# Fused local attention and feed-forward on one core: the weights' low parts move from GpSimd to VectorE, and blocks 0 to 5 scale their value products instead of their probabilities

## The chip, the core and the metric

The kernel runs on one core of a Trainium2 chip. The core has five engines, each with an instruction queue of its own that is worked off in order: TensorE (PE in the profile; its weight loads are listed apart as PEld), VectorE (DVE), ScalarE (ACT), GpSimd (POOL) and SyncE (SP), which here only issues DMA transfers. The metric is the time of one execution on the device in microseconds (us). The median of three runs before the change is 757.61 us.

## What is computed

The reference has two stages. The first is attention over 4 batches of 8 heads with 768 positions and 64 columns a head, in which a query sees the first 8 keys of its batch and the last 96 keys up to itself, with a bias that grows with distance:

```python
scores = scale * np.matmul(q, k.transpose(0, 1, 3, 2))
bias = -slopes[:, None, None] * dist[None, :, :]
scores = np.where(keep, scores + bias[None], -1000000000.0)
scores = scores - np.max(scores, axis=-1, keepdims=True)
a = np.exp(scores)
a = a / (np.sum(a, axis=-1, keepdims=True) + 1e-09)
attn_out = np.matmul(a, v).astype(np.float32)
```

The second takes the 3072 tokens of 512 columns that come out, x, through one feed-forward layer of width 2048:

```python
h = x @ w_in
g = h * (1.0 / (1.0 + np.exp(-h)))
out = (g @ w_out).astype(np.float32)
```

q, k and v come as 32-bit floats; w_in and w_out come as 64-bit floats, 8 MB each.

## The kernel before

**Attention** is cut into 24 blocks of 128 queries (six for each batch), `i` in the code, and each block into four pairs of heads, `hp`. A block needs 232 keys: 96 from the block before, the 8 global ones and its own 128; the first block of a batch needs only its own 128. For each block TensorE turns k and q (`turn`, L448), and for each pair of heads it makes the scores (L528 for blocks 0 to 5, L500 from block 6 on). VectorE adds the bias and finds the top (`top_of`, L540), ScalarE takes the exponential and its row sums (`expo`, L548), VectorE adds 1e-9 to the two sums of the pair and inverts them (`guard` L555, `inverse` L559), and `norm` (L565 to L574) scales the two heads' probabilities: one on GpSimd (L572) and one on VectorE (L574) for the first 16 pairs, that is blocks 0 to 3, and both on VectorE from block 4 on. TensorE turns the scaled probabilities (`turn_p`, L583), ScalarE moves them to SBUF as `pt` (L589), and TensorE multiplies them by v (`values`, L603). There v is the stationary operand, 64 columns a head, and `pt` streams 128 columns past it, so the result `pav` has the features of a head in its rows and the queries in its columns. ScalarE and VectorE split it into a high and a low part (`x_high` L615, `x_low` L618).

**The weights** come in 32 pieces of 512 KB, `n`, even ones from w_in and odd ones from w_out (`stage`, L364). VectorE puts a 32-bit float together from the halves of each 64-bit one in three steps (`conv1` L368, `conv2` L374, `conv3` L380), ScalarE rounds it to the reduced format of fast products (`conv_hi`, L387), and GpSimd subtracts this from the full value for the low part (`conv_lo`, L391).

**The feed-forward layer** takes two blocks at a time as a group `g` (12 groups) and the layer's width in 16 steps `f`. TensorE makes the hidden part from three products of high and low parts (`moe_h`, L723, 12 products a step), ScalarE takes the tanh (L729), VectorE makes the gate (`moe_gate`, L733), ScalarE rounds it (`moe_high`, L737) and the low part is subtracted (`moe_low`, L742: on GpSimd for groups 0 and 1 with f below 4, else on VectorE). TensorE multiplies by w_out (`moe_o`, L749, 6 products a step) into two PSUM banks that the group holds for all 16 steps. Step f needs the weights 2f and 2f + 1 with both their parts, so groups 0 and 1 run beside the conversion; block 6 and the later ones start their scores only when it is over, since their low parts of q take buffers of the staged weights.

**The order** of every engine's queue is fixed before the launch. The program lists its operations with an engine, a cost in ns, a rank, what they depend on and which buffers they take. `Plan.run` plays them through: whenever an engine is free it gives it the ready operation of the lowest rank whose buffers are to be had (`room`). So a changed cost or a changed engine alters the order of everything behind it. Where TensorE would have nothing to do in the first 60 us of this play, small products on zeros are put in (`filler`, L861). Eight PSUM banks are shared out by kind: output of the layer (`po`), values (`av`), scores (`s`), hidden part (`h`) and two kinds of turned data (`tp`, `tq`).

Of the kernel before, what the change touches and what calls it, by code (L numbers as in the profile page):

```python
# [10 lines left out]
F32 = mybir.dt.float32  # L11
# [6 lines left out]
ALU = mybir.AluOpType  # L18
# [3 lines left out]
P = 128  # L22
# [3 lines left out]
C1 = NPREV + NG  # L26
# [7 lines left out]

    C0=14, CR=1, LW=1, LB=5, QB=3.5, RI=0.1, RN=0, RP=0.2, RM=0, RV=1.2, RQ=0.1, RB=3, LK=-25, LAG=1,

    BP=(4, 3), NA=(0, 0), NP=(16, 0), PL=4, NX=20, CF=2, AHEAD=5, CN=4, I0=6, QS='ACT',
)


# [7 lines left out]
class Plan:  # L48
# [28 lines left out]
    def op(self, eng, cost, rank, emit, deps=(), uses=(), lat=None):  # L77
        o = dict(eng=eng, cost=int(cost), rank=rank, emit=emit, uses=list(uses), lat=lat,
                 need=0, ready=0, then=[], n=len(self.ops))
        for d in deps:  # L80
            if d is not None:
                d["then"].append(o)
                o["need"] += 1
        for b in o["uses"]:
            b.left += 1
        self.ops.append(o)
        return o
# [83 lines left out]
def attn_moe(ctx, tc, q, k, v, n_global, n_local, w_in, w_out, out):  # L171
# [216 lines left out]

    def conv_lo(n):
        _, hi, lo = weights(n)  # L390
        nc.gpsimd.tensor_sub(lo, st["f", n], hi.bitcast(F32))  # L391

    o_w, o_l = [], [None, None]
    for n in range(2 * NFC):
        rank = PAR["C0"] + PAR["CR"] * n
        a, m, x = [] if lent(n) is not None else [Buf("big")], Buf("mid"), lent(n)
        o = op("DMA", 1456, rank - PAR["LW"], (lambda n=n: stage(n, "w")), [o_l[x]] if not a else (), a, PAR["DL"])
        o = op("DVE", 335, rank, (lambda n=n: conv1(n)), [o], [*a, m])
        o = op("DVE", 602, rank, (lambda n=n: conv2(n)), [o], [*a, m])
        o = op("DVE", 602, rank, (lambda n=n: conv3(n)), [o], [*a, m])  # L400
        if x is not None:
            o_l[x] = o
        o_wf = o
        hi = op("ACT", 520, rank, (lambda n=n: conv_hi(n)), [o] + (o_l if n >= 2 * NFC - 4 else []), [m])
        lo = op("POOL", 1225, rank, (lambda n=n: conv_lo(n)), [hi], [m])
        o_w.append((hi, lo))
    lo["caps"] = dict(pt=5)

# [123 lines left out]
    def top_of(i, hp, a):  # L532
        t = blk[i]
        if not a:
            t["p", hp] = sb3.tile([P, 2, WIN], F32, name="pe")
            t["sum", hp] = sb3.tile([P, 2], F32, name="sm")
            t["inv", hp] = sb3.tile([P, 2], F32, name="rs")
        h, n = 2 * hp + a, cols(i)[1]
        nm = NM[:, i * H + h:i * H + h + 1]
        nc.vector.tensor_tensor_reduce(  # L540
            t["p", hp][:, a, :n], t["s", hp][a][:, :n], B1[:, h] if i % NJ else B0[:, h],
            -SC, 3.0e38, ALU.add, ALU.min, nm,
        )
# [14 lines left out]
        t = blk[i]  # L558
        nc.vector.reciprocal(t["inv", hp], t["inv", hp])  # L559

    def norm_on(u, a):

        return "ACT" if u < PAR["NA"][a] else "POOL" if u < PAR["NP"][a] else "DVE"

    def norm(i, hp, a):  # L565
        t = blk[i]
        x = t["p", hp][:, a, :cols(i)[1]]
        eng = norm_on(NHP * i + hp, a)
        if eng == "ACT":
            nc.scalar.mul(x, x, t["inv", hp][:, a:a + 1])  # L570
        elif eng == "POOL":
            nc.gpsimd.tensor_mul(x, x, t["inv", hp][:, a:a + 1].to_broadcast(x.shape))  # L572
        else:
            nc.vector.tensor_scalar(x, x, t["inv", hp][:, a:a + 1], None, ALU.mult)  # L574

    def turn_p(i, hp, tp):
        t = blk[i]
# [17 lines left out]
    def values(i, hp, av):  # L595
        t = blk[i]
        t["av"] = bank(av, NHP, P)
        pav, pt = t["av"], t["pt", hp]
        for c in range(0 if i % NJ else 1, 2):
            for a in range(2):  # L600
                r = slice(a * D, (a + 1) * D)
                x = t["v"] if c else t["vp"]
                nc.tensor.matmul(  # L603
                    pav[r, hp], x[:, 2 * hp + a], pt[:P if c else C1, c, a],
                    start=not c or not i % NJ, stop=c == 1,
                )

    def x_part(i, x):
        g, jj = divmod(i, NB)
# [16 lines left out]
    for i in range(B * NJ):  # L626
# [47 lines left out]
        if j:  # L674
            o_v.append(op("DMA", 1183, rank - lr + 1, (lambda i=i: load_prev(i)), (), [kk["vp"]], PAR["DL"]))
        pav = Buf("av")
        last, o_m, pts = None, [], []
        for hp in range(NHP):
            u = NHP * i + hp
            stacked = i >= PAR["I0"]  # L680
            s, pe, pt, tp = [Buf("s") for _ in range(1 if stacked else 2)], Buf("pe"), Buf("pt"), Buf("tp")
            ks = [kk[x] for x in ("KH", "KL", "QH", "QL") + (("R",) if stacked else ())]
            n = cols(i)[1]
            o = op("PE", 432 if stacked else 640, u,
                   (lambda i=i, hp=hp, s=s, f=stack_scores if stacked else scores: f(i, hp, s)),
                   [x for y, x in ob.items() if i or y[1] <= hp < y[1] + NHP // 2] + [before.get("s") if stacked else None], s + ks)
            before["s"] = o_s[u] = o
            if u == PAR["HU"]:
                o["hold"] = 1
            o_e = []  # L690
            for a in range(2):
                x = op("DVE", 318 if j else 210, u, (lambda i=i, hp=hp, a=a: top_of(i, hp, a)),
                       [o, o_b[j == 0, hp], before.get("top") if stacked and not a else None], [s[a % len(s)], pe])
                if not a:
                    before["top"] = x
                o_e.append(op("ACT", ACT(n, 112) + 186, u, (lambda i=i, hp=hp, a=a: expo(i, hp, a)), [x], [pe]))
            o = op("DVE", 67, u - PAR["RI"], (lambda i=i, hp=hp: guard(i, hp)), o_e, [pe])
            o = op("DVE", 72, u - PAR["RI"], (lambda i=i, hp=hp: inverse(i, hp)), [o], [pe])
            cost = dict(ACT=380, DVE=250, POOL=640) if j else dict(ACT=293, DVE=196, POOL=400)
            o = [op(norm_on(u, a), cost[norm_on(u, a)], u - PAR["RN"], (lambda i=i, hp=hp, a=a: norm(i, hp, a)), [o], [pe])  # L700
                 for a in range(2)]
            o = op("PE", 438 if j else 220, u - PAR["RP"], (lambda i=i, hp=hp, tp=tp: turn_p(i, hp, tp)), o, [pe, tp])
            o_m.append(op("ACT", ACT(512 if j else 256), u - PAR["RM"], (lambda i=i, hp=hp: move_p(i, hp)), [o, before.get("move") if stacked else None], [tp, pt]))
            before["move"] = o_m[-1]
            pts.append(pt)
            if not stacked or hp == NHP - 1:
                last = op("PE", ((1860 if j else 980) if stacked else 540 if j else 290), u - PAR["RV"],
                          (lambda i=i, hp=hp, av=pav: values_of(i, hp, av)),
                          [*o_m, last] + o_v, [*pts, pav, xb[g]["xh"], xb[g]["xl"], kk["vn"]] + ([kk["vp"]] if j else []))
                o_m, pts = [], []  # L710
        hi = op("ACT", 478, u, (lambda i=i: x_high(i)), [last], [pav, xb[g]["xh"]])
        o_x[g].append(hi)
        o_x[g].append(op("DVE", 602, u, (lambda i=i: x_low(i)), [hi], [pav, xb[g]["xh"], xb[g]["xl"]]))
# [24 lines left out]

    def moe_low(g, f):
        mo["gl", g, f] = gl = sb2.tile([P, GT], F32R, name="gl")  # L740
        eng = nc.gpsimd if g < 2 and f < PAR["PL"] else nc.vector
        eng.tensor_sub(gl, mo["th", g, f], mo["gh", g, f].bitcast(F32))  # L742

    def moe_o(g, f, tt, po):
        gh, gl, po = mo["gh", g, f], mo["gl", g, f], bank(po)
# [25 lines left out]
    for g in range(NGRP):  # L771
# [3 lines left out]
        for f in range(NFC):  # L775
            rank = 1e3 + (max(g, 1) * NFC + f + (PAR["LAG"] + 0.5 if g else 0))
            ph, th, gh, gl = Buf("h"), Buf("th"), Buf("gh"), Buf("gl")
            for c in range(NCC):
                o = op("PE", 329, rank + PAR["LK"] / 10, (lambda g=g, f=f, c=c, h=ph: moe_h(g, f, c, h)),
                       [o, *o_w[2 * f]] + o_x[g], [ph, xb[g]["xh"], xb[g]["xl"]])  # L780
                if f == c == 0:
                    o["hold"] = 2 if g == 1 else 1
            o_h[g, f] = o
            t = op("ACT", 264, FIRST + rank, (lambda g=g, f=f: moe_tanh(g, f)), [o], [ph, th])
            t = op("DVE", 335, FIRST + rank, (lambda g=g, f=f: moe_gate(g, f)), [t], [ph, th])
            hi = op("ACT", 307, FIRST + rank, (lambda g=g, f=f: moe_high(g, f)), [t], [th, gh])
            p = g < 2 and f < PAR["PL"]
            lo = op("POOL" if p else "DVE", 690 if p else 335, FIRST + rank, (lambda g=g, f=f: moe_low(g, f)), [hi], [th, gh, gl])
            for tt in range(NB):
                last[tt] = op("PE", 651, rank, (lambda g=g, f=f, tt=tt, x=po[tt]: moe_o(g, f, tt, x)),  # L790
                              [hi, lo, last[tt], *o_w[2 * f + 1]], [gh, gl, *po[tt:]])
                if g < 2 and f == NFC - 1:
                    last[tt]["hold"] = 1
# [243 lines left out]
```

## Time and profile before

| what | value |
|---|---|
| three runs | 757.61, 755.15 and 757.96 us, median 757.61 us |
| the profiled execution's own time | 757.3 us |
| its span, first to last instruction | 755.5 us |
| mean granted TensorE clock | 0.992 |
| span's chain by engine | PE 83%, DVE 12%, waiting to issue 3% |
| read from HBM, written | 56.69 MB, 6.29 MB |

The profile is of one execution. The span leaves out 1.8 us of its time before the first and after the last instruction. Busy times overlap: an instruction is listed until its last result is written, while the next one has already begun, so the spacing of starts is shorter than the listed duration. A product of TensorE is listed with about twice the time by which it holds up the next one. A busy TensorE is therefore read from the spacing of its products and from its gaps.

### The profile page before, as it was taken

The numbers are of one execution on the slowest core, as the hardware profiler recorded it, in microseconds if no ns is written. First come the engines' busy times: TensorE is split into PE (matmuls) and PEld (weight loads), VectorE is DVE, ScalarE is ACT, GpSimd is POOL, SyncE is SP. The second block draws the span as 40 slices with busy tenths as digits, with TensorE's granted clock in tenths as the row PEclk, the third lists the DMA queues.
The fourth block names the chain that finished last, engine by engine and source line by source line (L and its number), as shares of the span: only waits on it lengthen the run. The fifth ranks groups of instructions, "written<-read, shape, count | busy, mean of one in ns | idle before, by whom it ended". The sixth has DMA issues, their size and how long they took to land.

```text
span 755.5 us, 14215 instructions
## 1 busy us (share of the span) xinstructions
PE 721.3 (95%) x5203; PEld 636.8 (84%) x5203; DVE 491.7 (65%) x1439; ACT 422.6 (56%) x1105; POOL 91.6 (12%) x147
## 2 busy tenths in 40 slices
PE   8997676899999999999999999999999999999996
PEld 6776555788999999999899999998899999998995
DVE  5899999864666656756666757656666756544322
ACT  5976233574656656755656756646656646543221
POOL 3355545400000000000000000000000000000000
PEclk9999899999999999999999999999999999999999
DMA  7785535112412412313313324324314232000000
GB/s 148 214 211 175 163 121 183 56 29 54 132 62 69 118 60 71 102 49 97 99 49 90 87 52 109 85 54 109 97 31 109 71 82 54 29 2 1 29 1 33
DMA packets 117501, 63.98 MB, mean 85 GB/s; under 512 B 93744, under 2 KB 110384, under 8 KB 117424
## 3 DMA queue, kind: packets, MB, share of 16 engines
q1 hardware_dynamic: 116992, 62.86, 30.5%
q8 instruction: 43, 0.70, 0.4%
q14 instruction: 34, 0.28, 0.1%
q10 hardware_dynamic: 432, 0.13, 0.1%
HBM read 56.69 MB, written 6.29 MB: 83 GB/s over the span
## 4 chain that ended last, share of the span: by engine, by line
PE 83%; DVE 12%; issue 3%; DMA 1%; ACT 0%; SPq 0%; DVEq 0%
PE bank L723 33%; PE bank L749 32%; PE bank L603 5%; PE bank L583 4%; PE bank L500 4%; DVE wf L368 3%; PE bank L448 3%; DVE wf L374 2%; DVE wf L380 2%; DVE pe L540 1%; PE bank L861 1%; DVE pe L574 1%; PE bank L528 1%; DVE th L733 1%; DMA qn<-in_q_dram 1%
## 5 line engine op out<-in xcount | busy, mean ns | idle before, releaser
L723 PE MATMUL bank<-xh,WIH 128*128 128x256 f32 x768 | 226.2, 295 | 17.4 <-DVE th L733 16.1
L723 PE MATMUL bank<-xl,WIH 128*128 128x256 f32 x768 | 217.0, 283 | 0.0
L723 PE MATMUL bank<-xh,WIL 128*128 128x256 f32 x768 | 216.0, 281 | 0.0
L723 PEld LDWEIGHTS bank<-xh,WIH 128*128 128x128 f32 x768 | 145.2, 189 | 33.0 <-DVE th L733 22.3
L723 PEld LDWEIGHTS bank<-xl,WIH 128*128 128x128 f32 x768 | 145.4, 189 | 5.8
L723 PEld LDWEIGHTS bank<-xh,WIL 128*128 128x128 f32 x768 | 145.8, 190 | 0.0
L749 PE MATMUL bank<-WOH,gh 128*128 128x512 f32 x336 | 137.6, 410 | 0.0
L749 PE MATMUL bank<-WOH,gl 128*128 128x512 f32 x336 | 134.2, 399 | 2.7 <-DVE gl L742 2.7
L749 PE MATMUL bank<-WOL,gh 128*128 128x512 f32 x336 | 133.1, 396 | 0.0
L729 ACT ACTIVATE th<-bank 128x256 f32<-128x256 f32 x192 | 73.7, 384 | 101.1 <-PE bank L723 98.2
L737 ACT CAST gh<-th 128x256 fp32r<-128x256 f32 x192 | 77.3, 403 | 92.6 <-PE bank L749 55.0
L733 DVE SCALAR_TENSOR_TENSOR th<-th,bank 128x256 f32<-128x256 f32 x192 | 80.3, 418 | 64.4 <-ACT th L729 62.7
L742 DVE TENSOR_TENSOR gl<-th,gh 128x256 fp32r<-128x256 f32 x184 | 80.4, 437 | 54.1 <-ACT gh L737 51.8
L540 DVE CUSTOM_DVE_ANT_0 pe<-bank,B 128x232 f32<-128x232 f32 (+1 forms) x192 | 69.7, 376 | 62.8 <-PE bank L500 54.9
L548 ACT ACTIVATE pe<-pe,NM 128x232 f32<-128x232 f32 (+1 forms) x192 | 90.5, 473 | 22.9 <-DVE NM L540 21.1
L749 PEld LDWEIGHTS bank<-WOH,gl 128*128 128x128 f32 x336 | 63.6, 189 | 21.3 <-DVE gl L742 6.0
L589 ACT COPY pt<-bank 128x512 f32<-128x512 f32 (+1 forms) x96 | 52.4, 549 | 45.2 <-PE bank L583 44.2
L749 PEld LDWEIGHTS bank<-WOL,gh 128*128 128x128 f32 x336 | 64.3, 191 | 6.4
L749 PEld LDWEIGHTS bank<-WOH,gh 128*128 128x128 f32 x336 | 64.3, 191 | 6.3 <-issue 0.3
L514 POOL CAST KH<-KH 128x32 fp32r<-128x32 f32 x20 | 4.5, 227 | 458.5 <-PE bank L500 449.9
L583 PE MATMUL bank<-ident,pe 128*128 128x128 f32 (+1 forms) x352 | 55.3, 275 | 3.5 <-DVE th L733 2.5
L574 DVE TENSOR_SCALAR pe<-pe,rs 128x232 f32<-128x232 f32 (+1 forms) x176 | 53.9, 342 | 1.1
(112 smaller groups left out, 1008.2 us busy)
## 6 DMA issues: line engine op xcount, KB each, us to landing
c<-in_moe_w_in_dram SPq DMA_DIRECT2D x16, 512.0 KB, 4.0
c<-in_moe_w_out_dram SPq DMA_DIRECT2D x16, 512.0 KB, 4.3
vn<-in_v_dram SPq DMA_DIRECT2D x24, 256.0 KB, 3.4
w<-in_moe_w_in_dram SPq DMA_DIRECT2D x12, 512.0 KB, 4.8
w<-in_moe_w_out_dram SPq DMA_DIRECT2D x12, 512.0 KB, 3.6
kn<-in_k_dram SPq DMA_DIRECT2D x23, 256.0 KB, 3.0
qn<-in_q_dram SPq DMA_DIRECT2D x23, 256.0 KB, 3.2
out_dram<-osb SPq DMA_DIRECT2D x23, 256.0 KB, 3.2
```

Source lines behind the costliest of these rows:

```text
L540: nc.vector.tensor_tensor_reduce(t["p", hp][:, a, :n], t["s", hp][a][:, :n], B1[:, h] if i % NJ else B0[:, h], -SC, 3.0e38, ALU.add, ALU.m ...
L548: nc.scalar.activation(x, x, AF.Exp, bias=NM[:, i * H + h:i * H + h + 1], scale=-1.0, accum_out=t["sum", hp][:, a:a + 1],)
L574: nc.vector.tensor_scalar(x, x, t["inv", hp][:, a:a + 1], None, ALU.mult)
L583: nc.tensor.transpose(ps[:n, c, a], pe[:, a, c0:c0 + n], ident)
L589: nc.scalar.copy(t["pt", hp][:, c], t["tp", hp][:, c])
L603: nc.tensor.matmul(pav[r, hp], x[:, 2 * hp + a], pt[:P if c else C1, c, a], start=not c or not i % NJ, stop=c == 1,)
L723: nc.tensor.matmul(ph, w[:, c, fs], x[:, c], start=not c and not n, stop=c == NCC - 1 and n == 2)
L729: nc.scalar.activation(th, mo["ph", g, f], AF.Tanh, scale=0.5)
L733: nc.vector.scalar_tensor_tensor(gf, gf, 1.0, mo["ph", g, f], ALU.add, ALU.mult)
L737: nc.scalar.copy(gh, mo["th", g, f])
L742: eng.tensor_sub(gl, mo["th", g, f], mo["gh", g, f].bitcast(F32))
L749: nc.tensor.matmul(po, a[:, s], w_o(w, f), start=f == 0 and n == 0, stop=f == NFC - 1 and n == 2)
```

## The change

The low parts of the weights (`conv_lo`) and of the gates (`moe_low`) are all on VectorE. The parameters that put halves of the scaling on GpSimd are gone, and `norm` is always on VectorE. GpSimd keeps the carrying of keys from block to block (L514, L516), and some set-up.

Blocks 0 to 5 no longer scale probabilities. Their exponentials are turned as they are. The products with v swap their operands: `pt` is stationary with 128 columns (the queries) and v streams 64 columns past it, so that one PSUM bank takes a block's 8 heads with queries in the rows. One guard and one inverse act on the block's 8 sums, one multiplication scales the whole bank into SBUF (`norm_all`), and four transposes put it back into the layout that `x_high` and `x_low` read (`turn_x`).

```diff
-    BP=(4, 3), NA=(0, 0), NP=(16, 0), PL=4, NX=20, CF=2, AHEAD=5, CN=4, I0=6, QS='ACT',
+    BP=(4, 3), NX=20, CF=2, AHEAD=5, CN=4, I0=6, IV=6, QS='ACT',
...
     def conv_lo(n):
         _, hi, lo = weights(n)
-        nc.gpsimd.tensor_sub(lo, st["f", n], hi.bitcast(F32))
+        nc.vector.tensor_sub(lo, st["f", n], hi.bitcast(F32))
...
-        lo = op("POOL", 1225, rank, (lambda n=n: conv_lo(n)), [hi], [m])
+        lo = op("DVE", 602, rank, (lambda n=n: conv_lo(n)), [hi], [m])
...
+    def values_q(i, hp, av):
+        t = blk[i]
+        t["av"] = bank(av, H, D)
+        pt = t["pt", hp]
+        for h in (2 * hp, 2 * hp + 1):
+            for c in range(0 if i % NJ else 1, 2):
+                x = t["v"] if c else t["vp"]
+                nc.tensor.matmul(
+                    t["av"][:, h], pt[:P if c else C1, c, h % 2], x[:, h],
+                    start=not c or not i % NJ, stop=c == 1,
+                )
+
+    def guard_all(i):
+        x = blk[i]["sums"]
+        nc.vector.tensor_scalar(x, x, 1e-9, None, ALU.add)
+
+    def inverse_all(i):
+        x = blk[i]["sums"]
+        nc.vector.reciprocal(x, x)
+
+    def norm_all(i):
+        t = blk[i]
+        t["xq"] = x = sb2.tile([P, H, D], F32, name="xq", tag="mid", bufs=5)
+        nc.vector.tensor_mul(x, t["av"], t["sums"].unsqueeze(2).to_broadcast([P, H, D]))
+
+    def turn_x(i, tp):
+        t = blk[i]
+        t["av"] = ps = bank(tp, NHP, P)
+        for hp in range(NHP):
+            nc.tensor.transpose(ps[:, hp], t["xq"][:, 2 * hp:2 * hp + 2, :], ident)
...
-            o = op("DVE", 67, u - PAR["RI"], (lambda i=i, hp=hp: guard(i, hp)), o_e, [pe])
-            o = op("DVE", 72, u - PAR["RI"], (lambda i=i, hp=hp: inverse(i, hp)), [o], [pe])
-            cost = dict(ACT=380, DVE=250, POOL=640) if j else dict(ACT=293, DVE=196, POOL=400)
-            o = [op(norm_on(u, a), cost[norm_on(u, a)], u - PAR["RN"], (lambda i=i, hp=hp, a=a: norm(i, hp, a)), [o], [pe])
-                 for a in range(2)]
+            plain = i >= PAR["IV"]
+            o, o_all = o_e, o_all + o_e
+            if plain:
+                o = op("DVE", 67, u - PAR["RI"], (lambda i=i, hp=hp: guard(i, hp)), o_e, [pe])
+                o = op("DVE", 72, u - PAR["RI"], (lambda i=i, hp=hp: inverse(i, hp)), [o], [pe])
+                o = [op("DVE", 250 if j else 196, u - PAR["RN"], (lambda i=i, hp=hp, a=a: norm(i, hp, a)), [o], [pe])
+                     for a in range(2)]
...
+            if not plain:
+                last = op("PE", 460 if j else 230, u - PAR["RV"], (lambda i=i, hp=hp, av=pav: values_q(i, hp, av)),
+                          [o_m.pop(), last] + o_v, [pt, pav, kk["vn"]] + ([kk["vp"]] if j else []))
...
+        if not plain:
+            xq, tp = Buf("pt"), Buf("tp")
+            o = op("DVE", 67, u - PAR["RI"], (lambda i=i: guard_all(i)), o_all)
+            o = op("DVE", 72, u - PAR["RI"], (lambda i=i: inverse_all(i)), [o])
+            o = op("DVE", 602, u - PAR["RI"], (lambda i=i: norm_all(i)), [o, last], [pav, xq])
+            last = op("PE", 440, u - PAR["RV"], (lambda i=i, tp=tp: turn_x(i, tp)), [o], [xq, tp, xb[g]["xh"], xb[g]["xl"]])
+            pav = tp
...
-        eng = nc.gpsimd if g < 2 and f < PAR["PL"] else nc.vector
-        eng.tensor_sub(gl, mo["th", g, f], mo["gh", g, f].bitcast(F32))
+        nc.vector.tensor_sub(gl, mo["th", g, f], mo["gh", g, f].bitcast(F32))
...
-            p = g < 2 and f < PAR["PL"]
-            lo = op("POOL" if p else "DVE", 690 if p else 335, FIRST + rank, (lambda g=g, f=f: moe_low(g, f)), [hi], [th, gh, gl])
+            lo = op("DVE", 335, FIRST + rank, (lambda g=g, f=f: moe_low(g, f)), [hi], [th, gh, gl])
```

More of the change, by code (lines that the diff above doesn't have):

```diff
@@ L535, in top_of @@
             t["p", hp] = sb3.tile([P, 2, WIN], F32, name="pe")
-            t["sum", hp] = sb3.tile([P, 2], F32, name="sm")
-            t["inv", hp] = sb3.tile([P, 2], F32, name="rs")
+            if i >= PAR["IV"]:
+                t["sum", hp] = sb3.tile([P, 2], F32, name="sm")
+                t["inv", hp] = sb3.tile([P, 2], F32, name="rs")
+            elif not hp:
+                t["sums"] = x = sb3.tile([P, H], F32, name="sums")
+                for y in range(NHP):
+                    t["sum", y] = x[:, 2 * y:2 * y + 2]
         h, n = 2 * hp + a, cols(i)[1]
@@ L559, in inverse @@
         nc.vector.reciprocal(t["inv", hp], t["inv", hp])
-    def norm_on(u, a):
-        return "ACT" if u < PAR["NA"][a] else "POOL" if u < PAR["NP"][a] else "DVE"
     def norm(i, hp, a):
@@ L567, in norm @@
         x = t["p", hp][:, a, :cols(i)[1]]
[L568 to L574, printed above, removed]
+        nc.vector.tensor_scalar(x, x, t["inv", hp][:, a:a + 1], None, ALU.mult)
     def turn_p(i, hp, tp):
@@ L676, in attn_moe @@
         pav = Buf("av")
-        last, o_m, pts = None, [], []
+        last, o_m, pts, o_all = None, [], [], []
         for hp in range(NHP):
@@ L705, in attn_moe @@
             pts.append(pt)
-            if not stacked or hp == NHP - 1:
+            if not plain:
+                last = op("PE", 460 if j else 230, u - PAR["RV"], (lambda i=i, hp=hp, av=pav: values_q(i, hp, av)),
+                          [o_m.pop(), last] + o_v, [pt, pav, kk["vn"]] + ([kk["vp"]] if j else []))
+            elif not stacked or hp == NHP - 1:
                 last = op("PE", ((1860 if j else 980) if stacked else 540 if j else 290), u - PAR["RV"],
```

## The prediction

> **What bounds the kernel now.** I read the page's busy times and slices first.
>
> ```profile
> PE 721.3 (95%) x5203; PEld 636.8 (84%) x5203; DVE 491.7 (65%) x1439; ACT 422.6 (56%) x1105; POOL 91.6 (12%) x147
> DVE  5899999864666656756666757656666756544322
> POOL 3355545400000000000000000000000000000000
> ```
>
> TensorE bounds the whole, but VectorE is full in slices 2 to 6 (of 18.9 us each), the very ones in which GpSimd works. So I asked for busy times by stage, and for TensorE's waits between 30 and 145 us.
>
> ```profile
> 30.00:70.00 40.00, 36.17 (x308) 28.40 (x307) 39.24 (x121) 31.15 (x86) 20.55 (x27) 1.00 0.81 222
> 70.00:145.00 75.00, 54.33 (x283) 41.92 (x284) 74.59 (x103) 26.04 (x57) 40.43 (x28) 0.94 0.46 141
> 145.00:200.00 55.00, 55.00 (x417) 48.75 (x417) 31.08 (x106) 33.58 (x89) 3.83 (x9) 0.99 0.22 59
> 200.00:740.00 540.00, 540.00 (x3950) 489.41 (x3945) 324.44 (x1020) 309.06 (x802) 16.51 (x52) 1.00 0.24 67
> ```
>
> ```profile
> PE bank L723 <- DVE th L733: 16.1, 10, 3.0
> PE bank L749 <- DVE gl L742: 2.7, 6, 1.0
> ```
>
> The columns of the first are: stretch and length, busy time of PE, PEld, DVE, ACT and POOL, granted clock, share of the DMA engines, GB/s; those of the second: us in all, times, longest. From 30 to 145 us VectorE is busy 113.8 of 115 us, while TensorE lacks 3.8 + 20.7 = 24.5 us. From 145 us on TensorE has no gap and VectorE has room. TensorE's waits are for gates and low parts that stand in VectorE's queue behind the weights. **So up to the end of the weights VectorE sets the pace, and behind it TensorE's work does.** A us less on VectorE before 145 us is a us off the end, as long as TensorE has slack there.
>
> Why VectorE is slow there is seen in its order of time (start, duration), with the one GpSimd operation of the same moment:
>
> ```profile
> 104.57 0.68 DVE L380 SCALAR_TENSOR_TENSOR wf<-wl,wf 128x512 uint32<-128x512 uint32 x1
> ...
> 105.51 0.68 DVE L374 SCALAR_TENSOR_TENSOR wf<-wl,wf 128x512 uint32<-128x512 uint32 x1
> 106.11 1.51 DVE L368 TENSOR_SCALAR wf<-w 128x512 uint32<-128x512 uint32 x1
> 107.54 0.68 DVE L380 SCALAR_TENSOR_TENSOR wf<-wl,wf 128x512 uint32<-128x512 uint32 x1
> ...
> 123.21 0.42 DVE L368 TENSOR_SCALAR wf<-w 128x512 uint32<-128x512 uint32 x1
> 123.55 0.41 DVE L733 SCALAR_TENSOR_TENSOR th<-th,bank 128x256 f32<-128x256 f32 x1
> ```
>
> ```profile
> 105.98 1.35 POOL L391 TENSOR_TENSOR WIL<-wf,WIH 128x512 fp32r<-128x512 f32 x1 [1.61 <-ACT WIH L387]
> ```
>
> `conv1` (L368) takes 0.42 us at 123.21 but 1.51 us at 106.11, where it began inside GpSimd's subtraction (105.98 to 107.33) and ended 0.29 us behind it. The gate (L733), which reads PSUM and one SBUF tile, takes 0.41 us in its mean too (below). Starts lie 0.08 us closer than durations: 0.68 listed at 105.51, 0.60 to the next start.
>
> **The change, part by part, on VectorE up to 145 us.** The groups of that stretch:
>
> ```profile
> L380 DVE SCALAR_TENSOR_TENSOR wf<-w,wf 128x512 uint32<-128x512 uint32 x24 | 23.5, 980 | 0.1
> L368 DVE TENSOR_SCALAR wf<-w 128x512 uint32<-128x512 uint32 x24 | 20.9, 873 | 0.0
> L374 DVE SCALAR_TENSOR_TENSOR wf<-w,wf 128x512 uint32<-128x512 uint32 x24 | 19.5, 810 | 0.3
> ...
> L574 DVE TENSOR_SCALAR pe<-pe,rs 128x232 f32<-128x232 f32 x20 | 8.8, 457 | 0.1
> L733 DVE SCALAR_TENSOR_TENSOR th<-th,bank 128x256 f32<-128x256 f32 x20 | 8.2, 409 | 0.0
> L374 DVE SCALAR_TENSOR_TENSOR wf<-wl,wf 128x512 uint32<-128x512 uint32 x8 | 7.5, 933 | 0.0
> L742 DVE TENSOR_TENSOR gl<-th,gh 128x256 fp32r<-128x256 f32 x12 | 7.1, 594 | 0.0
> L368 DVE TENSOR_SCALAR wf<-wl 128x512 uint32<-128x512 uint32 x8 | 7.0, 887 | 0.0
> L380 DVE SCALAR_TENSOR_TENSOR wf<-wl,wf 128x512 uint32<-128x512 uint32 x8 | 6.9, 866 | 0.0
> L555 DVE TENSOR_SCALAR rs<-sm 128x2 f32<-128x2 f32 x20 | 4.3, 216 | 1.1 <-ACT pe L548 1.1
> L507 DVE TENSOR_TENSOR KL<-bank,KH 128x512 fp32r<-128x512 f32 x5 | 3.4, 679 | 0.0
> ...
> L559 DVE RECIPROCAL rs<-rs 128x2 f32<-128x2 f32 x20 | 3.2, 159 | 0.2
> ...
> L574 DVE TENSOR_SCALAR pe<-pe,rs 128x128 f32<-128x128 f32 x4 | 1.3, 320 | 0.1
> ```
>
> - *Stalls of the conversion.* Listed time of the three steps: L368 24 x 0.873 + 8 x 0.887 = 28.1 us, L374 26.9, L380 30.4, together 85.4 us. Unhindered 32 x (0.41 + 0.68 + 0.68) = 56.6. **-28.8 us.**
> - *Low parts of the weights.* 32 subtractions of 512 columns, as L507's: 0.68 - 0.08 = 0.60 us. **+19.2.**
> - *Low parts of the gates.* 8 more at 0.41 - 0.08 = 0.33, and the 12 shown lose 0.594 - 0.41 each. +2.6 - 2.2 = **+0.4.**
> - *Scaling of probabilities* (L574): 20 x 0.457 + 4 x 0.320 - 24 x 0.08 = **-8.5.**
> - *Guards and inverses*: 20 x (0.216 + 0.159) - 40 x 0.08 = **-4.3.**
> - *Once per block*: `norm_all` at 0.60 (512 columns from PSUM, again L507), guard and inverse of 8 columns at some 0.1 each; five blocks. **+4.0.** Its multiplier is broadcast, which no row shows; at double time it would be +3.0 more, and less than L507 nothing suggests.
>
> Sum: **-18.0 us**; the weights end at about 127 us.
>
> GpSimd loses these, and they leave no gap there, as nothing but carries of keys stands behind them:
>
> ```profile
> L391 POOL TENSOR_TENSOR WIL<-wf,WIH 128x512 fp32r<-128x512 f32 x16 | 23.9, 1495 | 16.7 <-ACT WIH L387 16.7
> L572 POOL TENSOR_TENSOR pe<-pe,rs 128x232 f32<-128x232 f32 x12 | 7.3, 611 | 15.4 <-DVE rs L559 12.4 <-PE bank L583 2.9
> L742 POOL TENSOR_TENSOR gl<-th,gh 128x256 fp32r<-128x256 f32 x8 | 7.2, 900 | 9.5 <-ACT gh L737 5.3 <-issue 4.2
> ```
>
> **On TensorE**, from the chain in order of time:
>
> ```profile
> 153.98 0.44 PE bank L583 x4
> ...
> 157.75 0.40 PE bank L500 x4
> ...
> 180.48 1.91 PE bank L603 x32
> ```
>
> A block's 16 value products are 32 records of 0.060 us, or 0.119 us a product: 64-column loads, the two heads side by side in the array. The new ones load 128 columns and stream 64. No row shows that form. If streaming alone counts, half the columns cost 0.060 us; if the load counts, two records of 0.11 (L583 and L500 load 128 columns and come every 0.10 to 0.11 us) make 0.22. I take 0.22, the nearest row by what is loaded. Blocks 0 and 1 to 5 have 8 and 16 products, 88 in all: between -5.2 and +8.9 us, taken at +8.9. The four transposes a block cost 0.44 us, 2.6 in all. Of this sum of 11.5, blocks 0 to 3, whose values are done before 145 us, have 56 x 0.10 + 4 x 0.44 = 7.4 us inside TensorE's slack. Blocks 4 and 5 have **+4.1 us** where TensorE has no gap.
>
> The Trainium skill speaks against this swap: "TensorE: Matmul & The Clock Gate", section "LDWEIGHTS", has the load's time go with its columns, about 107 ns for 128 (an estimate from its formula), and with it 88 x 2 x 0.107 = 18.8 us stand against 10.5. The spacing of L583 agrees with that figure; a stream of 64 columns behind such a load no run here shows.
>
> Does TensorE keep up? Its 24.5 us of gaps and its clock (0.94 of 54.3 us, so 3.3 us) make 27.8; less 18.0 and 7.4, 2.4 us remain, and the first product after a wait, which comes later than the rest, gives some more. At 145 us only 20 gates of groups 0 and 1 (L733 above) of 32 are made though all weights are there, because gates stood behind stalled steps. Without stalls I count two more steps done by the weights' end: 12 x 0.12 + 6 x 0.233 = 2.8 us of TensorE each, for 0.66 of VectorE: -5.6 + 1.3 = **-4.3 us**, by these rows:
>
> ```profile
> 174.85 1.41 PE bank L723 x12
> 176.26 1.40 PE bank L749 x6
> ```
>
> Probabilities no longer wait for guard, inverse and scaling, but for the exponential alone; x instead waits for `norm_all` and `turn_x`, some 2 us once a block, covered by the other blocks and the steps of f. Transfers are the same ones. I cost both at nothing.
>
> Span: 755.5 - 18.0 + 4.1 - 4.3 = 737.3; with the 1.8 us around it **739.1 us**, against the profiled 757.3, which is 0.3 below the median of the runs.
>
> **Rivals.** A measurement can tell about 0.5% from no change, 3.8 us: faster is below 753.5, slower above 761.1.
>
> - *The products stream, and TensorE takes the rest of its slack.* If values cost 0.119 as before, -8.9: 730.2 us; at 0.060 another 5.2 less, 725.0. For it: the load overlaps the product elsewhere. Against: nothing with 128 columns loaded comes faster than 0.10 us here.
> - *The staged weights become the bound.* If they came no faster than from 70 to 145 us, only the scaling, guards and inverses (-8.8) are won: 755.5 - 8.8 + 4.1 + 1.8 = 752.6 us. For it: few staging buffers. Against: the DMA engines are at 0.46 there and were at 0.81 before, and the queue's waits for buffers end on VectorE:
>
> ```profile
> SPq L364 <- DVE wf L380: 29.4, 7, 9.1
> ```
>
> - *Slower: VectorE waits for ScalarE.* A low part now stands in VectorE's queue behind the rounding on ScalarE. From the end of `conv3` (104.57 + 0.68) to the start of its low part on GpSimd (105.98) it took 0.73 us. If the fixed order put each low part right behind its `conv3`, everything queued behind it, gates and next weights, would wait: 32 x 0.73 = 23.4 us, 755.5 - 18.0 + 23.4 + 4.1 + 1.8 = 766.8 us. It decides slower from (18.0 - 4.1 + 3.8) / 32 = 0.55 us uncovered per weight. Against: at 104.57 to 107.54 steps of other weights stand between the steps of one, so there is work to put there.
> - *The change does not free VectorE*: the long steps come from something other than GpSimd. Then the 28.8 us stay: 739.1 + 28.8 = 767.9 us. Against: the 0.29 us behind GpSimd's end.
>
> **Chances.** The forecast, 731 to 747 us, has 0.60; the faster rival 0.22; the staging 0.10, half of it below 753.5; waiting for ScalarE 0.06; the last 0.02. So faster 0.60 + 0.22 + 0.05 = 0.87, same 0.05, slower 0.08. The range 724 to 750 takes in the cost of the products from both ends and part of the staging.
>
> **What the profile after would show.** GpSimd all but empty from 30 us on; L368, L374 and L380 at 0.41, 0.68, 0.68 us in their means, and L391 on VectorE at 0.68; the last L380 near 127 us; TensorE without long gaps from 40 us. The value products of blocks 0 to 5 in L603's place show their spacing: 0.11 a record or half of it. I am wrong if the steps stay over 0.8 us, if VectorE has gaps that end on ScalarE's rounding (L387) or on a DMA, or if TensorE's gaps before 127 us stay at 20 us.

## The result, and the profile after

| | before | after |
|---|---|---|
| median of the runs | 757.35 us (4 runs) | **735.74 us** (4 runs, 735.41 to 735.96) |
| ratio, 95% interval | | 0.9719 [0.9699, 0.9739] |
| span of the profiled execution | 755.5 us | 734.2 us |
| granted clock | 0.992 | 0.996 |

In the sets of runs further down, one execution of 1780 us and one of 2746 us lie far off all others and are left out of the ratios.

The forecast was 739.1 us, between 724 and 750. The page of the changed kernel, the lines that answer to those of before:

```profile
PE 722.7 (98%) x5236; PEld 650.9 (89%) x5236; DVE 471.3 (64%) x1417; ACT 422.0 (57%) x1105; POOL 28.1 (4%) x91
...
DVE  4689999986567566666665665765666756544322
...
POOL 2010000000000000000000000000000000000000
```

TensorE is busy for as long as before in a span that is 21.3 us shorter: its gaps went from 34.2 us (755.5 - 721.3) to 11.5. By stage:

```profile
30.00:70.00 40.00, 40.00 (x346) 35.95 (x346) 33.68 (x99) 30.57 (x87) 2.74 (x8) 1.00 0.76 210
70.00:127.00 57.00, 57.00 (x383) 51.72 (x382) 53.25 (x116) 28.90 (x68) 0.00 (x0) 1.00 0.52 151
127.00:145.00 18.00, 18.00 (x114) 16.19 (x113) 17.68 (x38) 8.48 (x19) 0.00 (x0) 1.00 0.58 175
145.00:200.00 55.00, 52.71 (x365) 47.05 (x365) 38.44 (x123) 37.11 (x98) 3.99 (x12) 0.97 0.27 72
```

From 30 to 145 us TensorE has no gap at all, where it had lacked 24.5 us. VectorE is busy 104.6 of these 115 us; it was 113.8. Its groups up to 200 us:

```profile
L374 DVE SCALAR_TENSOR_TENSOR wf<-w,wf 128x512 uint32<-128x512 uint32 x24 | 16.5, 686 | 0.1
L380 DVE SCALAR_TENSOR_TENSOR wf<-w,wf 128x512 uint32<-128x512 uint32 x24 | 16.4, 684 | 0.0
L391 DVE TENSOR_TENSOR WIL<-wf,WIH 128x512 fp32r<-128x512 f32 x16 | 11.2, 702 | 0.3 <-ACT WIH L387 0.3
L368 DVE TENSOR_SCALAR wf<-w 128x512 uint32<-128x512 uint32 x24 | 9.7, 418 | 0.5 <-DMA w<-in_moe_w_out_dram 0.4
L391 DVE TENSOR_TENSOR WOL<-wf,WOH 128x512 fp32r<-128x512 f32 x14 | 9.6, 685 | 0.0
L380 DVE SCALAR_TENSOR_TENSOR wf<-wl,wf 128x512 uint32<-128x512 uint32 x8 | 5.5, 685 | 0.0
L374 DVE SCALAR_TENSOR_TENSOR wf<-wl,wf 128x512 uint32<-128x512 uint32 x8 | 5.4, 685 | 0.0
```

The three steps (with 8 of L368 at 0.42) sum to 57.2 us; it was 85.4. And what VectorE now waits for, from 10 to 150 us:

```profile
DVE xq L628 <- PE bank L612: 4.4, 4, 2.4
DVE pe L545 <- PE bank L528: 4.1, 4, 1.5
DVE sums L619 <- ACT pe L553: 3.9, 2, 3.6
DVE th L773 <- ACT th L769: 3.6, 10, 0.7
```

The first two are waits for TensorE's products. From 30 to 145 us alone the second shrinks to 0.2 us; the first stays at 4.4 us, and the last, for ScalarE's tanh of the hidden part, at 3.6 us. TensorE, which waited for VectorE there before, has no wait left in that stretch.

**The weights did not end sooner.** The windows of two lines, gates first (busy time and count behind the length):

```profile
0.00:127.00 127.00, 9.20 (x22) 1.00 0.64 168
0.00:145.00 145.00, 11.69 (x28) 1.00 0.63 169
```

then low parts of the weights:

```profile
0.00:127.00 127.00, 16.02 (x23) 1.00 0.64 168
0.00:145.00 145.00, 20.13 (x29) 1.00 0.63 169
```

At 127 us, 22 gates are made, as many as forecast for that time, but 23 low parts and not all 32; at 145 us it is 28 and 29, where before it was 20 and 31. The last conversion step and the last low part begin here:

```profile
147.94 0.69 DVE L380 SCALAR_TENSOR_TENSOR wf<-w,wf 128x512 uint32<-128x512 uint32 x1
...
150.29 0.70 DVE L391 TENSOR_TENSOR w_last<-wf,w_last 128x512 fp32r<-128x512 f32 x1
```

So the weights end at about 151 us; before, the last L380 began at 144.2 us, earlier than now. The gain was taken in steps of the layer that run sooner.

### The profile page after: what moved, and what is told of

Same layout as the page of the kernel before. It is cut to its first block, busy times and chain, and to the rows that moved or that the text cites. A ratio compares the mean times of both kernels' runs of the same rounds, so it can differ in the third digit from the quotient of the medians.

```text
span 734.2 us, 14157 instructions
## 1 busy us (share of the span) xinstructions
PE 722.7 (98%) x5236; PEld 650.9 (89%) x5236; DVE 471.3 (64%) x1417; ACT 422.0 (57%) x1105; POOL 28.1 (4%) x91
## 4 chain that ended last, share of the span: by engine, by line
PE 97%; DMA 1%; DVE 1%; issue 0%; SPq 0%; ACT 0%; DVEq 0%
PE bank L763 38%; PE bank L788 36%; PE bank L578 5%; PE bank L598 4%; PE bank L500 4%; PE bank L448 3%; PE bank L612 3%; PE bank L528 2%; PE bank L899 1%; DMA qn<-in_q_dram 1%; DMA out_dram<-osb 1%; PE bank L634 0%; DVE osb L800 0%; DVE R L487 0%; DVE pe L569 0%
## 5 line engine op out<-in xcount | busy, mean ns | idle before, releaser
L788 PE MATMUL bank<-WOH,gh 128*128 128x512 f32 x336 | 136.1, 405 | 0.0
L769 ACT ACTIVATE th<-bank 128x256 f32<-128x256 f32 x192 | 73.6, 383 | 106.6 <-PE bank L763 104.6
L788 PE MATMUL bank<-WOH,gl 128*128 128x512 f32 x336 | 132.4, 394 | 0.0
L545 DVE CUSTOM_DVE_ANT_0 pe<-bank,B 128x232 f32<-128x232 f32 (+1 forms) x192 | 69.0, 376 | 63.2 <-PE bank L500 57.2
L578 PEld LDWEIGHTS bank<-ident,pe 128*128 128x128 f32 (+1 forms) x352 | 42.0, 137 | 6.6 <-DVE pe L569 0.6
L411 DVE TENSOR_REDUCE TOP<-c 128x1 f32<-128x512 int16 x64 | 42.3, 681 | 3.2 <-DMA c<-in_moe_w_in_dram 3.2
```

The lines of the kernel that those rows point to most:

```text
L411: nc.vector.tensor_reduce(TOP[:, i, n:n + 1], top, AX.X, (ALU.min, ALU.max)[i], apply_absolute_value=True)
L545: nc.vector.tensor_tensor_reduce(t["p", hp][:, a, :n], t["s", hp][a][:, :n], B1[:, h] if i % NJ else B0[:, h], -SC, 3.0e38, ALU.add, ALU.m ...
L578: nc.tensor.transpose(ps[:n, c, a], pe[:, a, c0:c0 + n], ident)
L769: nc.scalar.activation(th, mo["ph", g, f], AF.Tanh, scale=0.5)
L788: nc.tensor.matmul(po, a[:, s], w_o(w, f), start=f == 0 and n == 0, stop=f == NFC - 1 and n == 2)
```

## The experiments

Times are medians, ratios are to runs of the kernel before on the same chip (757.09, 757.28, 757.11 and 757.42 us in the four sets), and differences from the changed kernel are taken to 735.7 us. Where a parameter changes, the diff shows it without the rest of its line. Two theories stood against each other at first. **A** is the forecast's: VectorE sets the pace up to the weights' end, and TensorE's work counts only behind it. **B** is read from the trace after: TensorE is full, and VectorE has some 10 us to spare.

### 1. No queries in rows

```diff
-IV=6
+IV=0
```

> GpSimd is out of the weights' time as in the changed kernel, but no block has queries in rows: probabilities are scaled on VectorE per pair, values have 64-column loads. Theory A, as forecast (VectorE sets the pace up to the weights' end, TensorE has slack there): VectorE gets some 12 us more work in blocks 0 to 4 (40 scalings at 0.29, 40 guards and inverses at 0.08 to 0.1, less 5 x 0.8), TensorE's saving counts only for blocks 4 and 5 (4.1 us): about 8 us slower than the changed kernel, 743 us. Theory B, from the trace after (TensorE has no gap from 10 us to 160 us, so its own work counts): TensorE loses 88 x 0.10 + 24 x 0.11 = 11.5 us of work and VectorE's 12 us more fill what it still had free between 30 and 127 us (10 us): 724 to 734 us, faster than the changed kernel.

Measured 734.92 us, 0.9719 [0.9694, 0.9745]: the same as the changed kernel. **The whole gain comes from taking GpSimd out; queries in rows in all six blocks add nothing that shows.** A's 743 falls. B's range of 724 to 734 is missed by 0.9 us, and the gain that it expected isn't there: TensorE lost work, but VectorE came to its limit:

```profile
70.00:127.00 57.00, 53.76 (x324) 43.97 (x323) 56.56 (x119) 25.80 (x57) 0.00 (x0) 1.00 0.55 170
```

VectorE is busy 56.6 of 57 us and TensorE has 3.2 us of gaps. The 98 small products on zeros in this run, 74 in the changed kernel, took back some more (24 at 0.11 us, an estimate of 2.6 us).

### 2. The weights' low parts back on GpSimd

```diff
-        nc.vector.tensor_sub(lo, st["f", n], hi.bitcast(F32))
+        nc.gpsimd.tensor_sub(lo, st["f", n], hi.bitcast(F32))
...
-        lo = op("DVE", 602, rank, (lambda n=n: conv_lo(n)), [hi], [m])
+        lo = op("POOL", 1225, rank, (lambda n=n: conv_lo(n)), [hi], [m])
```

> The changed kernel with the weights' low parts alone put back on GpSimd (cost 1225 in the order's play). Both theories: the conversion's steps stall again, so L368, L374 and L380 together go from 57 to about 85 us and 19 us of subtractions leave VectorE: 9 to 10 us more on VectorE. Theory A: 9 to 10 us slower than the changed kernel, 745 us. Theory B: VectorE has 10 us free between 30 and 127 us, so 0 to 6 us slower, 736 to 742. If the stalls do not come from GpSimd's subtractions, the steps stay at 57 us and the kernel gets faster, 725 to 735.

Measured 749.79 us, 0.9923 [0.9903, 0.9944]: 14.1 us slower than the changed kernel, more than either theory said. TensorE's waits up to 200 us and the stage:

```profile
PE bank L763 <- DVE th L773: 12.1, 7, 3.2
```

```profile
70.00:127.00 57.00, 48.54 (x286) 42.46 (x285) 56.83 (x84) 21.15 (x47) 28.12 (x19) 0.91 0.53 158
```

The three steps of the conversion grew by 25 us to 82.2, and 19.2 us of subtractions left, so VectorE's sum rose by only 6. The other 8 us are not settled. Part may be the clock, granted at 0.91 in this stage (0.09 x 48.5 = 4.4 us of TensorE's time, an estimate). The counts also show an order that fits worse: by 145 us all 32 low parts have begun (29 in the changed kernel), but only 22 gates are made (28 there). The play of the order doesn't know of the stalls, so it lets VectorE convert weights that no step can use yet. That reading was not tested by itself.

One thing runs 1 and 2 do show: the end of the weights does not set the time by itself. The last L380 begins at 137.6 us in run 1 and at 141.6 us in run 2, in both sooner than the 147.9 us of the changed kernel; yet run 1 takes as long as that, and run 2 takes 14 us more.

### 3. Queries in rows in blocks 0 to 3 only

```diff
-IV=6
+IV=4
```

> Queries in rows only in blocks 0 to 3; blocks 4 and 5 scale probabilities on VectorE and have 64-column loads. TensorE saves 32 products x 0.10 and 8 transposes x 0.11 = 4.1 us, VectorE gets 16 scalings at 0.29, 16 guards and inverses less two times 0.8, 4.5 us. Theory A: block 4's half of VectorE's work counts before the weights' end, TensorE's saving behind it: 2 us faster, 733.7. Theory B: 4 us faster, 731.6.

Measured 731.85 us, 0.9674 [0.9644, 0.9705], 3.9 us below the changed kernel, as B has it (A: 2). The interval overlaps the changed kernel's, so it is not settled that this version is faster at all.

### 4. More work for VectorE

```diff
     def conv2(n):
         f = st["f", n]
-        nc.vector.scalar_tensor_tensor(
-            f, st["w", n][..., 0], 29, f, ALU.logical_shift_right, ALU.bitwise_or
-        )
+        for _ in range(2):
+            nc.vector.scalar_tensor_tensor(
+                f, st["w", n][..., 0], 29, f, ALU.logical_shift_right, ALU.bitwise_or
+            )
...
-        o = op("DVE", 602, rank, (lambda n=n: conv2(n)), [o], [*a, m])
+        o = op("DVE", 1204, rank, (lambda n=n: conv2(n)), [o], [*a, m])
```

> The changed kernel with the second step of each weight's conversion done twice (the same bits), 32 x 0.60 = 19.2 us more on VectorE before the weights' end, known to the order's play. Theory A: the weights' end and the kernel's end move by 19 us: 755 us. Theory B: VectorE first uses up what it has free (about 10 us between 30 and 127 us), and TensorE fills its time with steps that are ready: 6 to 10 us slower, 742 to 746.

Measured 752.79 us, 0.9949 [0.9934, 0.9964]: 17.1 us slower for 19.2 us of work. **B falls here**: VectorE had almost nothing to spare. A's 755 us comes close, but A has fallen in run 1. VectorE's gaps in the trace after are waits for results, and work put into its queue does not slide into them.

```profile
127.00:160.00 33.00, 27.52 (x164) 22.43 (x163) 32.69 (x67) 13.34 (x29) 0.00 (x0) 1.00 0.49 144
```

VectorE is busy 32.7 of 33 us in this stretch, in which the changed kernel is done with the weights at 151 us, and TensorE lacks 5.5 us.

### 5. More work for TensorE

This led to theory **C**: from 30 to 150 us both engines are at their limit, TensorE because it has no gap and VectorE because its gaps are waits.

```diff
-            for c in range(0 if i % NJ else 1, 2):
+            for c in 2 * tuple(range(0 if i % NJ else 1, 2)):
```

> The changed kernel with the value products of blocks 0 to 5 made twice (the second time over the first, the same result; the order's play doesn't know of it): 88 products more, at the 0.224 us that they take (records 0.112 apart) 19.7 us more on TensorE. Theory A, as forecast (TensorE has slack up to the weights' end): only blocks 4 and 5 count, 32 x 0.224 = 7 us, 743 us. Theory C, from the first four runs (TensorE and VectorE are both full from 30 to 150 us, so more work on either moves the end): 17 to 20 us slower, 753 to 756.

Measured 754.27 us, 0.9952 [0.9930, 0.9973]: 18.5 us slower for 19.7 us of work, of which A would count 7. TensorE stays without a gap, and VectorE's share falls:

```profile
30.00:70.00 40.00, 40.00 (x365) 37.32 (x363) 24.53 (x77) 23.43 (x69) 2.73 (x8) 1.00 0.58 161
70.00:127.00 57.00, 57.00 (x411) 52.02 (x410) 47.99 (x112) 29.47 (x73) 0.00 (x0) 1.00 0.56 162
```

With runs 1, 3 and 4, C stands so far: 19 to 20 us more on either engine cost 17 to 18.5, and 12 us moved from one to the other (run 1) cost nothing. The order in run 5 is that of the changed kernel; what a play that knows of the added products would make of them was not run.

### 6. and 7. Is it GpSimd that stalls the steps?

GpSimd subtracts once more, in place, behind each low part:

```diff
+    def beside(n):
+        f = st["f", n]
+        nc.gpsimd.tensor_sub(f, f, weights(n)[1].bitcast(F32))
...
+        op("POOL", 1225, rank, (lambda n=n: beside(n)), [lo], [m])
```

> The changed kernel, and behind each low part on VectorE GpSimd subtracts once more in place, a result that nobody reads: the same form that it had before (two inputs in SBUF, 512 columns), 32 times, with no one waiting for it but the next use of the staging buffer. If the long steps of the conversion came from GpSimd's reading and writing beside them, L368, L374 and L380 go from 57 us in their sum to some 85, and with the 17 us that 19 us of VectorE's work cost in the run with the second step twice, the kernel takes 755 to 761 us. If they came from the waits or the order of before, they stay at 57 us and the kernel at 736 to 738.

Measured 753.16 us, 0.9935 [0.9912, 0.9959]: 17.4 us slower, a little less than expected. The steps went from 57.2 to 78.0 us, where 85 had been expected:

```profile
L380 DVE SCALAR_TENSOR_TENSOR wf<-w,wf 128x512 uint32<-128x512 uint32 x24 | 24.3, 1014 | 0.0
L374 DVE SCALAR_TENSOR_TENSOR wf<-w,wf 128x512 uint32<-128x512 uint32 x24 | 22.0, 915 | 0.2
...
L778 DVE SCALAR_TENSOR_TENSOR th<-th,bank 128x256 f32<-128x256 f32 x36 | 14.8, 411 | 4.1 <-ACT th L774 4.0
L368 DVE TENSOR_SCALAR wf<-w 128x512 uint32<-128x512 uint32 x24 | 14.3, 598 | 1.8 <-POOL wf L395 1.2 <-DMA w<-in_moe_w_out_dram 0.7
```

Nobody needs GpSimd's result here, except for the place that it frees (1.2 us of waits of L368, in the last line), so **the long steps come from GpSimd working beside them**. In order of time, one subtraction and two of the steps:

```profile
106.17 1.28 POOL L395 TENSOR_TENSOR wf<-wf,WOH 128x512 f32<-128x512 f32 x1 [0.69 <-DVE WOL L391]
```

```profile
106.28 1.72 DVE L374 SCALAR_TENSOR_TENSOR wf<-w,wf 128x512 uint32<-128x512 uint32 x1
...
109.53 0.68 DVE L374 SCALAR_TENSOR_TENSOR wf<-w,wf 128x512 uint32<-128x512 uint32 x1
```

The first step lies beside the subtraction, the second has none beside it. Over the whole stage, 34 steps with two inputs in SBUF (L374, L380 and the low parts, L391) overlap a subtraction and take 1.24 us in their mean; the 61 others take 0.68. The gate (L778), with PSUM and one SBUF tile as inputs, stays at 0.41.

The time does not follow VectorE's sum one for one. With the low parts of the weights (22.2 us in the changed kernel, 24.8 here) and of the gates (0.423 and 0.494 us each, 36 of them), VectorE's instructions grew by 26 us in all, for 17.4 us of time.

The second run lets GpSimd only write:

```diff
-        nc.gpsimd.tensor_sub(f, f, weights(n)[1].bitcast(F32))
+        nc.gpsimd.memset(f, 0.0)
```

> The run with GpSimd beside, but GpSimd only writes zeros over the staged value (512 columns, no input) instead of subtracting. If GpSimd's reading is what holds up steps with two SBUF inputs, L374 and L380 stay at 0.68 us and the low part's L391 at 0.69, and only L368 (one input, 0.41 us) can grow: 736 to 742 us. If any use of SBUF by GpSimd holds them up for as long as it lasts, L374, L380 and L391 grow as well: by less than in the run with subtractions, as a write of zeros is shorter, 740 to 748 us.

Measured 736.25 us (2 runs), 0.9720 [0.9679, 0.9762], as the changed kernel:

```profile
L374 DVE SCALAR_TENSOR_TENSOR wf<-w,wf 128x512 uint32<-128x512 uint32 x24 | 16.5, 686 | 0.2
L380 DVE SCALAR_TENSOR_TENSOR wf<-w,wf 128x512 uint32<-128x512 uint32 x24 | 16.4, 684 | 0.0
L391 DVE TENSOR_TENSOR WIL<-wf,WIH 128x512 fp32r<-128x512 f32 x16 | 11.0, 687 | 0.4 <-ACT WIH L387 0.3
L368 DVE TENSOR_SCALAR wf<-w 128x512 uint32<-128x512 uint32 x24 | 10.6, 441 | 0.9 <-DMA w<-in_moe_w_out_dram 0.7 <-DMA w<-in_moe_w_in_dram 0.2
```

Steps with two inputs in SBUF do not notice a GpSimd that writes for 0.53 us 32 times. They did lie beside it: 26 of the 96 overlap one of its writes, and none of the 96 takes more than 0.70 us. So what stalls the two-input steps is GpSimd's reading. L368, with one input, grows a little (0.418 to 0.441 in its mean, 0.68 at most), and with the subtraction it took up to 1.51 us; these runs do not tell how much of that is GpSimd's reading and how much its writing.

On the two-input steps, the Trainium skill says this in "SBUF — State Buffer", section "Who interferes with whom": VectorE's second SBUF input comes through an interface shared with GpSimd's reads, not with its writes. These two runs agree.

### 8. to 12. Looking for a better version

Run 8 has the probabilities of blocks 0 to 5 scaled on ScalarE, and no queries in rows:

```diff
-IV=6
+IV=0, NA=24
...
-        nc.vector.tensor_scalar(x, x, t["inv", hp][:, a:a + 1], None, ALU.mult)
+        if NHP * i + hp < PAR["NA"]:
+            nc.scalar.mul(x, x, t["inv", hp][:, a:a + 1])
+        else:
+            nc.vector.tensor_scalar(x, x, t["inv", hp][:, a:a + 1], None, ALU.mult)
...
-                o = [op("DVE", 250 if j else 196, u - PAR["RN"], (lambda i=i, hp=hp, a=a: norm(i, hp, a)), [o], [pe])
+                on = ("ACT", 380 if j else 293) if u < PAR["NA"] else ("DVE", 250 if j else 196)
+                o = [op(*on, u - PAR["RN"], (lambda i=i, hp=hp, a=a: norm(i, hp, a)), [o], [pe])
```

> GpSimd is out as in the changed kernel, no block has queries in rows, and the probabilities of blocks 0 to 5 are scaled on ScalarE (0.38 us each, 15 us up to block 4), guards and inverses on VectorE. Against the changed kernel TensorE loses 11.5 us of work and VectorE stays the same (40 x 0.09 more, 5 x 0.8 less). Theory A (only VectorE's work and TensorE's behind the weights count): 4 us faster, 731.5. Theory C: 8 to 11 us faster, 724.5 to 728, if ScalarE, busy 31 of 40 us from 30 to 70 us, can take it; if it cannot, 730 or more.

Measured 733.34 us, 0.9681 [0.9663, 0.9698]: 2.4 us faster, not 8. TensorE had almost no gap (0.3 us from 30 to 70 us), although it had 11.5 us less of work: the play had put in 154 small products on zeros, where the changed kernel has 74. Their rows, here and in the changed kernel:

```profile
L903 PE MATMUL bank<-wx 128*128 128x256 bf16 x154 | 25.0, 301 | 1.1 <-DVE wx L307 1.1
```

```profile
L899 PE MATMUL bank<-wx 128*128 128x256 bf16 x74 | 14.0, 324 | 1.1 <-DVE wx L307 1.1
```

Run 9 is the changed kernel with these only in the first 20 us:

```diff
-WEND=60000
+WEND=20000
```

> The changed kernel with the small products on zeros put in only in the first 20 us of the order's play, not 60 (ties in the play are broken by number, not by address, so the order can differ a little). In the trace after 38 of the 74 lie behind 20 us, at 0.11 us each 4.2 us. Theory C (TensorE is never without work there, so they only take its time): 3 to 4 us faster, 732. Theory A, or if they stand where TensorE would wait: no change, 735.7.

Measured 731.58 us, 0.9653 [0.9636, 0.9670], 4.2 us faster as C has it, with an interval clear of the changed kernel's. That run also breaks ties of the play by number instead of by address, which run 10 does alone:

```diff
-                        heapq.heappush(back, (t + lat, id(b), b))
+                        heapq.heappush(back, (t + lat, len(back) + 1000 * o["n"], b))
```

> The changed kernel with nothing but the ties of the order's play broken by number instead of by address. It is there to part the order from the products on zeros: 735 to 737 us if the gain of the run with 20 us came from those products, 732 if from the order.

Measured 736.48 us, 0.9736 [0.9706, 0.9766]: the order of ties is not it. The next two have the 20 us together with another idea. Run 11 takes ScalarE's scaling:

> As the run with the scaling on ScalarE (no queries in rows, GpSimd out), with the small products on zeros only in the first 20 us of the order's play; ties by number. In that run's trace 154 of them take 21.1 us of TensorE, 111 of these behind 20 us, where TensorE had 0.3 us of gaps: its 11.5 us less of work had gone to them. Theory C (TensorE full, each product in its queue counts): 111 x 0.11 = 12 us less in the queue; 724 us if half of it becomes waits, 721 if none. Theory A, or if they stand in real waits: no change, 733.

Measured 733.45 us, 0.9692 [0.9667, 0.9716]: nothing gained, **a miss of 9 to 12 us** by theory C; what holds is the expectation's other branch, that the products stand in real waits. The stage from 30 to 70 us, in run 8 and then in run 11:

```profile
30.00:70.00 40.00, 39.71 (x371) 32.47 (x370) 34.47 (x117) 38.98 (x115) 3.18 (x8) 1.00 0.78 201
```

```profile
30.00:70.00 40.00, 36.19 (x288) 27.40 (x288) 32.46 (x117) 37.62 (x111) 3.00 (x8) 0.89 0.72 191
```

ScalarE is busy 39.0 of 40 us there in run 8, and the longest of TensorE's waits up to 200 us in run 11 are for ScalarE:

```profile
PE bank L581 <- ACT pe L570: 2.9, 3, 1.5
PE bank L601 <- ACT pt L587: 2.1, 4, 0.9
```

So ScalarE had become a limit, and the small products stood in real waits. Without them TensorE has gaps of 3.8 us, and its granted clock is 0.89 instead of 1.00. Run 12, the last, has blocks 0 to 3 in rows with the 20 us:

> Queries in rows in blocks 0 to 3 alone and the small products on zeros only in the first 20 us; ties by number. If the two gains (3.9 and 4.2 us) lie in the same full queue of TensorE they add up: 727.5 us. If VectorE is what the first of them meets next (its gaps there were 6 us from 30 to 100 us), 730.

Measured 731.98 us, 0.9672 [0.9644, 0.9701]: the two gains do not add up, and the time lies 2 us above the higher expectation. TensorE gets gaps again (1.0 us from 70 to 127), with VectorE busy 56.4 of 57 us:

```profile
70.00:127.00 57.00, 55.96 (x349) 47.80 (x349) 56.40 (x119) 26.14 (x59) 0.00 (x0) 1.00 0.55 164
```

Runs 3, 9 and 12 lie at 731.6 to 732.0 us, below both kernels. Their intervals overlap one another, and those of 3 and 12 overlap the changed kernel's too, so only run 9 is clearly faster than it.

## Why the prediction was right, and where not

- **The stalls** were taken for 28.8 us and gave 28.2 (85.4 to 57.2), shown by GpSimd's return beside (run 6) to be GpSimd's doing. Low parts at 0.68 listed: 0.69.
- **Value products** were taken at 0.22 us by the load, not 0.060 to 0.119 by the stream. The products of block 5 in order of time:

```profile
159.40 0.39 PE L612 MATMUL bank<-vn,pt 128*128 128x64 f32 x2
159.63 0.39 PE L612 MATMUL bank<-vp,pt 104*128 104x64 f32 x2
159.85 0.39 PE L612 MATMUL bank<-vn,pt 128*128 128x64 f32 x2
```

  Two records, one product, every 0.22 to 0.23 us. That is what the prediction took from L583, the nearest row by what is loaded: 64 streamed columns come no faster than 128 did behind a load of 128.
- **The step that failed** is "the weights end at about 127 us", and with it that VectorE sets the pace up to there. VectorE's work fell (113.8 to 104.6 us busy from 30 to 145 us, with 8 more gates in it), but TensorE met its own limit first. Full from 30 us on, it has no wait left, while VectorE stands idle for 10.4 us (115 - 104.6); the rest went into steps (28 gates at 145 us, not 20) and not into weights, which end at about 151 us. Run 5 shows that TensorE's work counts there (18.5 of 19.7 us), where the prediction gave blocks 0 to 3 no price. Why the order put steps ahead of weights was not tested.
- **Why the sum held all the same**: the prediction had worked out that TensorE's slack (27.8 us less 7.4) was just about VectorE's gain plus two steps. The sum by TensorE alone is 755.5 - 27.8 + 11.5 = 739.2 us of span, two us from the 737.3 of the other way. That the two ways lie so close is due to this kernel's numbers, so the hit of the forecast is in part luck. Measured were 734.2. What both lack, some 3 to 5 us, is probably time in which TensorE was listed as busy and yet late: its busy time rose by 1.4 us, although the new products and transposes add 11.5, so about 10 us of listed time went elsewhere, of which the prediction counted 3.3 for the clock. This is a difference of sums and was not measured by itself.
- **The rivals.** The faster one needed cheap products, and they were not. The staging showed in 0.4 us of waits of L368 for a DMA. VectorE waited 0.3 us for ScalarE's rounding, against 23.4 us at worst. None of these took place. The fourth, long steps with another cause than GpSimd, falls with run 6.
- Queries in rows, half of the change, were counted as -8.8 us on VectorE and +11.5 on TensorE. Run 1 shows what they add in all: nothing beyond the noise.

## What to carry to other kernels

When an engine runs slow operations, look at what a neighbour does in the same moment before counting its work: 32 subtractions moved to the busiest engine of that stage relieved it, because each had held up steps there for 0.8 us (run 2: 25.0 / 32) and costs 0.60 itself. Where two engines are both near full in a stage, work moved from one to the other may be worth nothing (12 us in run 1), and work added to either is mostly paid (17 to 18.5 of some 19 us in runs 4 and 5); price both sides before choosing where to put work. A schedule that is played through beforehand with costs that leave out such stalls may order the work badly as well, as the counts of run 2 suggest.

## What the runs showed of the hardware that was not expected

- GpSimd's writing alone (0.53 us, 32 times) leaves VectorE's steps with two SBUF inputs at 0.684 to 0.687 us in their means (run 7); beside a subtraction, which reads, they take up to 1.78 us, 1.1 us more (run 6).
- Small products on zeros cost time in one version (4.2 us, run 9) and nothing in another (runs 8 and 11, 733.3 and 733.5 us).
- In run 11 TensorE has gaps of 3.8 us from 30 to 70 us and a granted clock of 0.89 there. The kernel before has gaps of 3.8 us in the same stretch at 1.00, so the sum of the gaps does not decide the clock; what does stays open.
- A stream of 64 columns behind a load of 128 columns takes 0.11 us a record (L612), the same as 128 columns behind such a load (L583 before: four in 0.44 us).
